# Preparing the next block's tokens earlier: the load in the first pair's value pass, the four sums two and two

## The chip, the cores and the metric

The kernel runs on one core of one Trainium2 chip. The metric is the time of one execution in device microseconds, as a median of several runs. One execution is also recorded by the hardware profiler; its rows are what this document reads. The engines are named as in the rows: PE is TensorE's matrix multiplication, PEld its weight load, DVE is VectorE, ACT is ScalarE, POOL is GpSimd, and SP is SyncE, whose queue issues all the DMAs here.

## The reference

Eight sequences of 3008 tokens with 256 channels go through a spectral mixing layer and then through a gated network. The part around the change is the second one:

```python
X = np.fft.rfft(x, axis=1)                 # then complex 256 x 256 mixing, soft threshold
y = np.fft.irfft(Y, n=x.shape[1], axis=1)
x = y.reshape(24064, 256)
g = x @ w_gate                             # 256 x 1536
silu = g * (1.0 / (1.0 + np.exp(-g)))
val = x @ w_val                            # 256 x 1536
return (silu * val @ w_out).astype(np.float32)   # 1536 x 256
```

## The kernel before

**Two stages.** A first stage of some 680 us does the transforms (by matrix multiplications) and writes the mixed tokens, channels first, to `xt_d` in DRAM. The second stage, `gated_ffn`, fills the rest. It is the stage that the change touches.

**Blocks, pairs, passes.** The second stage runs over 24 blocks of tokens: 22 of 2 x 512 tokens and two of 2 x 384 (`BLOCKS`). Each block runs over six pairs (`q` = 0 to 5) of 256 hidden columns, and each pair has a gate pass (`n` = 0) and a value pass (`n` = 1). In this text the first pair is q = 0 and blocks count from 0.

**Seven products in place of eight.** A pass multiplies a 2 x 2 split of the weights (two halves of the channels, two of the hidden columns) with the 2 x 2 split of the tokens (two halves of the channels, two of the tokens) by a scheme with seven block products, so the operands are seven sums and differences of the quarters. Each product is made of three multiplications, since each operand is split into a high part and a low part, the remainder (`product`, line 516). The gate pass also runs three, the value pass four of the seven products of the down projection of the pair before (`down`).

**Who makes the operands.** For the up projection, `x_sum` (line 502) makes four further operands in place in the token tile `xf`, each a subtraction on GpSimd. `x_part` then makes the high part on ScalarE (line 510) and the low part on GpSimd (line 511), seven times per block. For the down projection, the quarters H11, H12, H22, H21 lie in `hidden`; VectorE makes four differences T1 to T4 in `more` (`diff`, line 527), ScalarE the high parts (`upper`, line 532) and GpSimd the low parts (`lower`, line 536). Seven such low parts fall to a pair: T1, H11 and H22 in the value pass, and H21, T3, T2 and T4 in the gate pass that follows.

**The order.** In the second stage the order on TensorE, VectorE, ScalarE and GpSimd is the order in which the program is written (`manual_schedule`). SyncE's queue is not in that list; the framework's planner orders its requests. Preparation of block b + 1 is woven into block b through a table: `later(ahead, q, n, after, fn)` calls `fn` in pass (q, n) of the block ahead, after the up product numbered `after` (1, 5, 6, 2, 7, 3, 4 is the order in a pass). In a value pass, what stands "after 6" comes on GpSimd's queue behind the low part of T1 and in front of those of H11 and H22.

**The token tile.** There is one tile `xf` (one buffer). `load_x(blk)` may overwrite it once the last of the seven `x_part` of the block before has read it; these stand in the value passes of the fourth pair (two), the fifth (two) and the sixth (three). The weights of the up projection come pass by pass in a ring of four tiles, requested by `load_unit` at the start of each pass for the pass three further on (line 480).

**The inverse pieces.** In blocks 1 to 16 a last piece of the inverse transform is worked off: `inverse` puts eight small multiplications into the gate pass of the third pair, behind ScalarE's reading of the first bank.

Of the kernel before, what the change touches and what calls it, by code (L numbers as in the profile page):

```python
# [120 lines left out]
@with_exitstack  # L121
def spectral_ffn(ctx: ExitStack, tc: tile.TileContext, xp, w_r, w_i, cb, wup_raw, wdn_raw, ca, cf, ci, co, out):
    nc = tc.nc
    const = ctx.enter_context(tc.tile_pool(name="const", bufs=1))
    dram = ctx.enter_context(tc.tile_pool(name="dram", bufs=2, space=DRAM))
    wdn = [const.tile([P, NQ, 7, P], F32R, name=f"wdn_{p}") for p in ("hi", "lo")]
    ring = ctx.enter_context(tc.tile_pool(name="ring", bufs=RING, reuse_waits="tile"))
    xt_d = [dram.tile([P, 2, SEQ], F32, name=f"xt_d{b}", bufs=1) for b in range(B)]
    d2 = {B - 1: dram.tile([NK, P, C], F32, name="d2_last", bufs=1)}
    wup_d = [dram.tile([P, 2, 7 * P], F32, name=f"wup_d{u}", bufs=1) for u in range(2 * NQ)]  # L130


    front = ctx.enter_context(tc.tile_pool(name="front", bufs=1))
    ps_ = ctx.enter_context(tc.tile_pool(name="ps", bufs=1, space=PSUM))

    with ExitStack() as tail:
        last = tail.enter_context(tc.tile_pool(name="last", bufs=2, side="right"))
        with ExitStack() as one:
            finish = transform(one, tc, front, last, ps_, xp, w_r, w_i, cb, wup_raw, wdn_raw, ca, cf, ci, co, wdn, wup_d, xt_d, d2)
        finish()  # L140
        ffn = gated_ffn(ctx, tc, front, ring, ps_, co, wdn, wup_d, xt_d, d2[B - 1], out)
        next(ffn)
    next(ffn, None)
# [319 lines left out]
def gated_ffn(ctx, tc, front, ring, ps_, co, wdn, wup_d, xt_d, d2, out):  # L463
# [22 lines left out]
    def load_x(blk):  # L486
        s, h = BLOCKS[blk]
        end = s + 2 * h
        raw = raws[blk] = front.tile(XF, F32, name="xf", tag="xf").rearrange("p a b -> p (a b)")[:, : 8 * h].rearrange("p (a b) -> p a b", b=h)
        x4 = raw[:, :4, :].rearrange("p a b -> p (a b)").rearrange("p (cc t) -> p cc t", cc=2)  # L490
        at = 0
        while s < end:
            b, off = divmod(s, SEQ)
            n = min(SEQ - off, end - s)
            nc.sync.dma_start(x4[:, :, at : at + n], xt_d[b][:, :, off : off + n])
            s += n
            at += n
        xs[blk] = {}

    def x_sum(blk, o, a, b):  # L500
        f = lambda i: raws[blk][:, i, :]
        g.tensor_tensor(f(o), f(a), f(b), op=ALU.subtract)

    SUMS = ((4, 0, 1), (6, 2, 4), (5, 2, 0), (7, 3, 6))

    def x_part(blk, n_):
        h = BLOCKS[blk][1]
        src = raws[blk][:, X_AT[n_], :]
        part = xs[blk][n_] = sb.tile([P, 2, T], F32R, name="x_parts", bufs=12)
        act.copy(part[:, 0, :h], src)  # L510
        g.tensor_tensor(part[:, 1, :h], src, f32(part[:, 0, :h]), op=ALU.subtract)  # L511
# [209 lines left out]
    def later(blk, q, n, after, fn):  # L721
        todo.setdefault((blk, q, n), {}).setdefault(after, []).append(fn)

    for blk in range(1, len(BLOCKS)):
        ahead = blk - 1
        order = list(X_AT)
        later(ahead, 1, 0, 1, lambda blk=blk: load_x(blk))
        for i, (q, n) in enumerate(((2, 1), (2, 1), (2, 1), (3, 1))):
            later(ahead, q, n, 6, lambda blk=blk, i=i: x_sum(blk, *SUMS[i]))
        for n_, (q, after) in zip(order, ((3, 6), (3, 6), (4, 6), (4, 6), (5, 1), (5, 5), (5, 6))):  # L730
            later(ahead, q, 1, after, lambda blk=blk, n_=n_: x_part(blk, n_))
    for blk, u in pieces.items():
# [86 lines left out]
```

## Time and profile before

| what | value |
|---|---|
| median of 3 runs | 2769.14 us (2768.75 to 2771.31) |
| time of the profiled execution | 2764.52 us |
| its span, first to last instruction | 2762.6 us |
| mean granted TensorE clock | 0.991 |
| TensorE busy | 2684.7 us (97%) |
| VectorE, ScalarE, GpSimd busy | 2157.9, 1718.8, 2096.8 us (78%, 62%, 76%) |

A busy share is an average over the whole span. In the rows of a timeline, the first number is the start of an instruction in microseconds from the span's start, the second the time that it and its like took; "x3" is three in a row, and the bracket is the time in which the engine was idle just before, with what ended it.

### The profile page before, as it was taken

The page shows a single profiled execution, that of the slowest core. Times are in us where ns is not written, and L with a number is a line of the kernel's source. Part 1 is how long each engine was busy: PE and PEld are TensorE (multiplying, and loading weights), DVE is VectorE, ACT ScalarE, POOL GpSimd, SP SyncE. Part 2 cuts the span into 40 slices and gives each one's busy share as a digit, 9 for nine tenths or more (in the row PEclk, how much of TensorE's full clock was granted, in tenths as well). Part 3 has the DMA queues.
Part 4 walks back from the last instruction along what each step waited for, and adds up shares of the span by engine and source line. Part 5 has one row for each costly group of instructions (what it writes and reads, how often), then busy time and mean ns, then how long its engine had stood idle before and what let it go on. Part 6 is the DMA issues. An engine that isn't in the chain of part 4 may idle for free. (4 is left out here: it accounts for less than half of the span.)

```text
span 2762.6 us, 39633 instructions
## 1 busy us (share of the span) xinstructions
PE 2684.7 (97%) x13173; PEld 2200.4 (80%) x13173; DVE 2157.9 (78%) x2916; ACT 1718.8 (62%) x3280; POOL 2096.8 (76%) x1574
## 2 busy tenths in 40 slices
PE   8999999889999999999999999999999999999998
PEld 5777787787888888888888888888888888888898
DVE  3777677774788888888788878888788888888887
ACT  4666666666656665666665665666666666666665
POOL 1555556554888888888888898889888898888885
PEclk9999999999999999999999999999999999999999
DMA  8889987765344444444444444454444444444453
GB/s 248 263 269 296 305 295 245 235 208 181 134 162 158 155 151 146 167 157 152 139 160 169 152 153 144 159 169 140 148 161 155 162 141 144 152 163 149 148 179 108
DMA packets 180124, 491.88 MB, mean 178 GB/s; under 512 B 17264, under 2 KB 89584, under 8 KB 179824
## 3 DMA queue, kind: packets, MB, share of 16 engines
q1 hardware_dynamic: 179920, 489.35, 53.5%
q8 instruction: 105, 1.72, 0.3%
q14 instruction: 99, 0.81, 0.1%
HBM read 378.65 MB, written 110.62 MB: 177 GB/s over the span
## 5 line engine op out<-in xcount | busy, mean ns | idle before, releaser
L516 PE MATMUL bank<-x_parts,wup 128*128 128x512 f32 (+1 forms) x6048 | 1530.6, 387 | 1.2 <-POOL x_parts L511 0.7
L516 PEld LDWEIGHTS bank<-x_parts,wup 128*128 128x128 f32 x6048 | 1122.6, 188 | 239.2 <-DVE bank L645 22.3
L536 POOL TENSOR_TENSOR h_parts<-more,h_parts 128x512 fp32r<-128x512 f32 (+1 forms) x573 | 846.3, 1492 | 97.8 <-ACT h_parts L532 84.2
L536 POOL TENSOR_TENSOR h_parts<-hidden,h_parts 128x512 fp32r<-128x512 f32 (+1 forms) x432 | 602.9, 1408 | 210.1 <-ACT h_parts L532 167.3
L516 PE MATMUL bank<-h_parts,wdn_hi 128*128 128x512 f32 (+1 forms) x2016 | 627.2, 389 | 2.1 <-POOL h_parts L536 0.9
L532 ACT CAST h_parts<-hidden 128x512 fp32r<-128x512 f32 (+1 forms) x432 | 265.1, 614 | 451.8 <-DVE hidden L618 451.8
L516 PEld LDWEIGHTS bank<-h_parts,wdn_hi 128*128 128x128 f32 x2016 | 378.1, 188 | 97.3 <-POOL h_parts L536 26.3
L618 DVE TENSOR_TENSOR hidden<-hidden,bank 128x512 f32<-128x512 f32 (+1 forms) x576 | 375.9, 674 | 77.8 <-PE bank L516 69.2
L557 DVE TENSOR_TENSOR sums<-sums,bank 128x512 f32<-128x512 f32 (+1 forms) x360 | 241.8, 672 | 228.5 <-PE bank L516 228.4
L532 ACT CAST h_parts<-more 128x512 fp32r<-128x512 f32 (+1 forms) x576 | 351.7, 611 | 103.6 <-DVE more L527 94.9
L516 PE MATMUL bank<-h_parts,wdn_lo 128*128 128x512 f32 (+1 forms) x1008 | 388.9, 386 | 4.2 <-DVE sums L557 4.2
L527 DVE TENSOR_TENSOR more<-hidden 128x512 f32<-128x512 f32 (+1 forms) x288 | 341.0, 1222 | 0.0
L616 ACT ACTIVATE hidden<-bank 128x512 f32<-128x512 f32 (+1 forms) x432 | 252.1, 583 | 85.5 <-PE bank L516 79.4
L527 DVE TENSOR_TENSOR more<-hidden,more 128x512 f32<-128x512 f32 (+1 forms) x288 | 284.5, 988 | 0.0
L351 POOL TENSOR_TENSOR t<-t,y 128x512 f32<-128x512 f32 x96 | 132.5, 1380 | 132.6 <-DVE y L350 132.6
L623 ACT COPY bank<-bank 128x512 f32<-128x512 f32 (+1 forms) x288 | 161.6, 561 | 109.4 <-DVE hidden L618 104.0
L645 DVE TENSOR_TENSOR bank<-hidden,bank 128x512 f32<-128x512 f32 (+1 forms) x288 | 196.3, 681 | 37.2 <-PE bank L516 27.4
L516 PEld LDWEIGHTS bank<-h_parts,wdn_lo 128*128 128x128 f32 x1008 | 189.5, 188 | 41.2 <-issue 4.5
L511 POOL TENSOR_TENSOR x_parts<-xf,x_parts 128x512 fp32r<-128x512 f32 (+1 forms) x168 | 210.5, 1272 | 11.5 <-PE bank L516 7.1
L316 POOL TENSOR_TENSOR f<-f 128x256 f32<-128x256 f32 x96 | 84.0, 875 | 149.7 <-ACT f L315 146.7
L631 ACT COPY hidden<-bank 128x512 f32<-128x512 f32 (+1 forms) x288 | 167.3, 581 | 2.6
L349 ACT COPY t<-mixb 64x256 f32<-64x256 f32 x384 | 140.6, 366 | 25.9 <-PE mixb L337 16.2
(94 smaller groups left out, 3280.4 us busy)
## 6 DMA issues: line engine op xcount, KB each, us to landing
wup<-wup_d SPq DMA_DIRECT2D x288, 896.0 KB, 4.6
d<-a SPq DMA_DIRECT2D x128, 192.0 KB, 4.3
a_in<-d SPq DMA_DIRECT2D x96, 256.0 KB, 4.4
out<-o SPq DMA_DIRECT2D x88, 256.0 KB, 6.1
scratch<-xp SPq DMA_DIRECT2D x116, 192.0 KB, 4.8
d<-z SPq DMA_DIRECT2D x84, 256.0 KB, 3.9
z_in<-d SPq DMA_DIRECT2D x56, 384.0 KB, 5.2
xt_d<-xt SPq DMA_DIRECT2D x56, 376.0 KB, 4.4
```

Of the source, the lines that this page charges most:

```text
L349: nc.scalar.copy(t[64 * half : 64 * half + 64, k * C : (k + 1) * C], mixb[64 * k : 64 * k + 64, half * C : (half + 1) * C])
L511: g.tensor_tensor(part[:, 1, :h], src, f32(part[:, 0, :h]), op=ALU.subtract)
L516: nc.tensor.matmul(o, lhsT=weights[w], rhs=parts[x], start=start and i == 0, stop=stop and i == 2, skip_group_check=True)
L527: v.tensor_tensor(at(o, h), at(a, h), at(b, h), op=ALU.subtract)
L532: act.copy(pair[i][:, 0, :h], at(i, h))
L536: eng.tensor_tensor(pair[i][:, 1, :h], at(i, h), f32(pair[i][:, 0, :h]), op=ALU.subtract)
L557: v.tensor_tensor(o, o, spare[:, :h], op=ALU.add)
L616: act.activation(at(i, h), src, AF.Silu)
L618: v.tensor_tensor(at(i, h), at(i, h), src, op=ALU.mult)
L623: act.copy(b3[:, :h], b1[:, :h])
L631: act.copy(m5, b2[:, :h])
L645: v.tensor_tensor(b2[:, :h], m5, b3[:, :h], op=ALU.add)
```

## The change

Three lines of the table `later` change. The load of the next block's tokens moves from the gate pass of the second pair to the value pass of the first. The four sums, which stood as three in the value pass of the third pair and one in that of the fourth, now stand as two in the value pass of the second pair and two in that of the third. Their place in the pass (after product 6) and their own order stay, as do the seven token parts.

```diff
     for blk in range(1, len(BLOCKS)):
         ahead = blk - 1
         order = list(X_AT)
-        later(ahead, 1, 0, 1, lambda blk=blk: load_x(blk))
-        for i, (q, n) in enumerate(((2, 1), (2, 1), (2, 1), (3, 1))):
-            later(ahead, q, n, 6, lambda blk=blk, i=i: x_sum(blk, *SUMS[i]))
+        later(ahead, 0, 1, 1, lambda blk=blk: load_x(blk))
+        for i, q in enumerate((1, 1, 2, 2)):
+            later(ahead, q, 1, 6, lambda blk=blk, i=i: x_sum(blk, *SUMS[i]))
         for n_, (q, after) in zip(order, ((3, 6), (3, 6), (4, 6), (4, 6), (5, 1), (5, 5), (5, 6))):
             later(ahead, q, 1, after, lambda blk=blk, n_=n_: x_part(blk, n_))
```

## Rows read from the trace of the kernel before

**Rows 1.** The page: busy time of each engine, share of the span, instructions.
```profile
PE 2684.7 (97%) x13173; PEld 2200.4 (80%) x13173; DVE 2157.9 (78%) x2916; ACT 1718.8 (62%) x3280; POOL 2096.8 (76%) x1574
```

**Rows 2.** Waits of PEld, 700 to 2741 us: total us, times, longest us.
```profile
PEld bank L516 <- POOL h_parts L536: 24.7, 69, 0.5
PEld bank L516 <- DVE bank L645: 21.5, 66, 0.4
```

**Rows 3.** Timeline of ACT: line 623 at the start of blocks 1, 17, 21, 22.
```profile
765.02 0.57 ACT L623 COPY bank<-bank 128x512 f32<-128x512 f32 x1 [0.74 <-DVE hidden L618]
...
2177.19 0.57 ACT L623 COPY bank<-bank 128x512 f32<-128x512 f32 x1 [0.74 <-DVE hidden L618]
...
2525.59 0.57 ACT L623 COPY bank<-bank 128x512 f32<-128x512 f32 x1 [0.74 <-DVE hidden L618]
...
2611.38 0.46 ACT L623 COPY bank<-bank 128x384 f32<-128x384 f32 x1 [0.74 <-DVE hidden L618]
```

**Rows 4.** Timeline of ACT, block 19: line 623 opening pairs three to six.
```profile
2380.18 0.57 ACT L623 COPY bank<-bank 128x512 f32<-128x512 f32 x1 [0.74 <-DVE hidden L618]
...
2394.45 0.57 ACT L623 COPY bank<-bank 128x512 f32<-128x512 f32 x1 [0.74 <-DVE hidden L618]
...
2409.45 0.57 ACT L623 COPY bank<-bank 128x512 f32<-128x512 f32 x1 [0.74 <-DVE hidden L618]
...
2424.28 0.57 ACT L623 COPY bank<-bank 128x512 f32<-128x512 f32 x1 [0.74 <-DVE hidden L618]
```

**Rows 5.** Timeline of POOL, block 19, from the third pair's value pass.
```profile
2390.01 3.93 POOL L502 TENSOR_TENSOR xf<-xf 128x512 f32<-128x512 f32 x3
2393.90 4.70 POOL L536 TENSOR_TENSOR h_parts<-hidden,h_parts 128x512 fp32r<-128x512 f32 x3
```

**Rows 6.** Timeline of PEld, block 19, fourth pair's gate pass.
```profile
2395.24 0.19 PEld L516 LDWEIGHTS bank<-h_parts,wdn_hi 128*128 128x128 f32 x1 [0.21 <-POOL h_parts L536]
...
2396.94 0.19 PEld L516 LDWEIGHTS bank<-h_parts,wdn_hi 128*128 128x128 f32 x1 [0.49 <-POOL h_parts L536]
...
2398.10 0.53 PEld L516 LDWEIGHTS bank<-x_parts,wup 128*128 128x128 f32 x3 [0.39 <-DVE bank L645]
```

**Rows 7.** Timeline of DVE, block 19: gate passes of pairs four and six.
```profile
2394.28 3.15 DVE L527 TENSOR_TENSOR more<-hidden 128x512 f32<-128x512 f32 x2
...
2424.11 1.95 DVE L527 TENSOR_TENSOR more<-hidden 128x512 f32<-128x512 f32 x2
2426.30 0.69 DVE L645 TENSOR_TENSOR bank<-hidden,bank 128x512 f32<-128x512 f32 x1 [0.24 <-PE bank L516]
```

**Rows 8.** Timeline of POOL, block 19, fifth pair's value pass and what follows.
```profile
2419.83 2.54 POOL L511 TENSOR_TENSOR x_parts<-xf,x_parts 128x512 fp32r<-128x512 f32 x2
2422.33 2.57 POOL L536 TENSOR_TENSOR h_parts<-hidden,h_parts 128x512 fp32r<-128x512 f32 x2
2426.05 1.30 POOL L536 TENSOR_TENSOR h_parts<-hidden,h_parts 128x512 fp32r<-128x512 f32 x1 [1.15 <-DVE more L527]
```

**Rows 9.** Timeline of POOL, block 19, second pair's value pass and what follows.
```profile
2377.42 1.29 POOL L536 TENSOR_TENSOR h_parts<-hidden,h_parts 128x512 fp32r<-128x512 f32 x1 [1.64 <-ACT h_parts L532]
2379.51 1.29 POOL L536 TENSOR_TENSOR h_parts<-hidden,h_parts 128x512 fp32r<-128x512 f32 x1 [0.81 <-ACT h_parts L532]
2381.94 1.29 POOL L536 TENSOR_TENSOR h_parts<-hidden,h_parts 128x512 fp32r<-128x512 f32 x1 [1.14 <-ACT h_parts L532]
```

**Rows 10.** Timeline of ACT, block 9: line 623 opening pairs three and four.
```profile
1499.73 0.57 ACT L623 COPY bank<-bank 128x512 f32<-128x512 f32 x1 [0.75 <-DVE hidden L618]
...
1515.26 0.57 ACT L623 COPY bank<-bank 128x512 f32<-128x512 f32 x1 [0.75 <-DVE hidden L618]
```

**Rows 11.** Timeline of SP around the start of block 20.
```profile
2437.78 0.32 SPq L480 DMA_DIRECT2D wup<-wup_d  x1
2438.15 0.83 SPq L495 DMA_DIRECT2D xf<-xt_d  x1
```

**Rows 12.** DMA issues: count, KB each, median us from issue to landing.
```profile
wup<-wup_d SPq DMA_DIRECT2D x288, 896.0 KB, 4.6
...
xf<-xt_d SPq DMA_DIRECT2D x15, 1024.0 KB, 6.9
```

## The prediction

> **What bounds the kernel now.** I read first the table of engines, then the waits of TensorE's weight loader, then the lengths of the passes, and last what each engine does inside the passes that are too long.
>
> TensorE is busy for 97% of the span [rows 1], so in the gated network nearly every microsecond is its own. What an edit of GpSimd's order can give back is only the time in which TensorE stands still for GpSimd. The waits of the weight loader over the gated network name two causes of nearly equal size: 69 waits for a low part that GpSimd makes (24.7 us), and 66 for the bank that VectorE adds at line 645 (21.5 us) [rows 2]. That is three of each per block in 22 blocks. These totals overstate the loss, since the loader runs ahead of the multiplications and makes up part of it; I therefore go by lengths.
>
> ScalarE's copy at line 623 runs once per pass, so the distance from one such copy to another is a length. The rows give the starts of blocks 1, 17, 21 and 22 (counted from 0) [rows 3]. Blocks 1 to 16 take (2177.19 - 765.02) / 16 = 88.26 us each. Blocks 17 to 20 take (2525.59 - 2177.19) / 4 = 87.10 us. Block 21 takes 2611.38 - 2525.59 = 85.79 us. Block 21 does the same multiplications on 512 columns, but the tokens that it prepares for its successor are only 384 wide. It is the control: a block whose GpSimd work fits.
>
> Inside a block between 17 and 20 the third pair takes 2394.45 - 2380.18 = 14.27 us, the fourth 15.00 and the fifth 14.83 [rows 4]. So the loss sits in the fourth and fifth pairs: 0.73 + 0.56 = 1.29 us, against 87.10 - 85.79 = 1.31 by the control.
>
> Why there: in the value pass of the third pair GpSimd does three sums in a row (3.93 us), and only then, back to back, three subtractions in 4.70 us [rows 5]. The first of these ends at about 2395.2, and the loader resumes at 2395.24 after 0.21 us of waiting for it; the second ends at about 2396.9, and the loader resumes at 2396.94 after 0.49 us; then it waits 0.39 us for VectorE's bank [rows 6]. VectorE is late as a consequence: two differences took it 3.15 us in that gate pass, where the gate pass behind only two extra instructions shows 1.95 us [rows 7]. The fourth pair's value pass has three extras too (one sum and two token parts), and the fifth pair pays 0.56 us. The fifth pair's value pass has exactly two extras, 2.54 us in all, and two subtractions follow in 2.57 us; after them GpSimd is already idle again for 1.15 us [rows 8]. Two extras fit; three do not.
>
> **The change, part by part.**
>
> *The sums.* Nothing is removed: 4 sums per block, about 3.93 / 3 = 1.31 us each [rows 5]. What changes is extras per value pass. Second to fifth pair, before: 0, 3, 3, 2. After: 2, 2, 2, 2. The last pair keeps its 3 token parts, which end the block and lie inside the control's 85.79 too.
>
> *The second pair's value pass, which gains two sums.* Today GpSimd is idle there for 1.64 us, 0.81 us and 1.14 us around three subtractions [rows 9]. The subtraction in front of the first gap is over at 2377.42 - 1.64 = 2375.8. Two sums follow to about 2378.4 (the second reads what the first wrote; I allow 0.1 us for it). The subtraction of H11 then runs until 2379.7, where it now ends at 2378.7. That of H22 starts at about 2379.7 instead of 2379.51 and ends near 2381.0, 0.1 to 0.2 us late. The next is due at 2381.94, so the delay is repaid before it. Is TensorE waiting by then? In the fourth pair, without its waits, the loader would have wanted H11 at 0.79 - 0.21 = 0.58 us after the pass began, and H22 at 2.49 - 0.49 - 0.21 = 1.79 us after it [rows 4, 6]. The third pair's gate pass begins at 2380.18 [rows 4]: H11 would be ready 0.5 us before that, H22 0.8 us after it, about 1 us of margin for each. I cost the two sums at nothing. The cover is that idle time; if it were gone, the cost would be what three extras cost, 0.73 us per block.
>
> *The third pair's value pass, which loses one of three sums,* becomes the same case: the fourth pair falls from 15.00 to about 14.27 us.
>
> *The fourth pair's value pass* keeps only two token parts, the case of [rows 8]: the fifth pair falls from 14.83 to 14.27 us.
>
> *The load.* It is written one pass earlier, and the only transfer that it is moved past is one request for weights. In the trace it already runs earlier than either place: SyncE's own order puts it at 2438.15, right behind the weight request at 2437.78 [rows 11], before the block even begins. It takes 6.9 us to land [rows 12], so the tokens are there by 2445.1. Pairs last 14.3 us, so the first sum in the new place comes some 24 us after the block's start at about 2438.5. Even if the load went out only at its written place, 7 us into the block, it would land with some 10 us in hand. A cost of nothing is the lower bound; the upper one is in the slower rival.
>
> *What is late next.* The blocks with an inverse piece (1 to 16) lose time of another kind: in one of them the third pair takes 1515.26 - 1499.73 = 15.53 us [rows 10], 1.26 us over 14.27. This is not touched by the change and stays. Without it these blocks take 88.26 - 1.26 = 87.00 us, 1.21 above the control.
>
> **The sum.** Blocks 1 to 16: 16 x 1.21 = 19.4 us. Blocks 17 to 20: 4 x 1.31 = 5.2 us. Blocks 0 and 22 also do full preparation (22 is narrower, preparing the same width); I take 1.3 each, 2.6 us. Together 27.2 us. The profiled execution took 2764.52 us and would take 2737.3; the median of the runs shown, 4.6 us higher at 2769.14, becomes 2742.
>
> **The rivals.**
>
> *The inverse piece meets the two sums* (chance 0.07). In blocks 1 to 16 the gate pass behind the moved sums also holds the inverse, whose multiplications stand in TensorE's own order. If the late H22 reaches it, the third pair pays what the fourth pays now: 16 x 0.73 = 11.7 us, a gain of 15.5 us, 2754 us. Against it: the margin of about 1 us.
>
> *VectorE is held by the later subtraction* (chance 0.08). The difference at the end of a value pass reads two SBUF tiles and slows beside GpSimd [rows 7]. If the 0.1 to 0.2 us by which H22 is late goes on to VectorE and from there to TensorE in the third and fourth pair, it costs up to 2 x 0.15 x 22 = 6.6 us: 2749 us. Against it: in the gate pass behind two extras VectorE still had 0.24 us to wait for TensorE [rows 7], which covers it. The Trainium skill, "SBUF — State Buffer", section "Who interferes with whom", says that a VectorE instruction with two SBUF inputs contends with a GpSimd instruction that reads SBUF and that the one issued first blocks the other for its whole length. By that rule sums added to a pass are a danger to VectorE's differences. The trace agrees that differences stretch (1.95 us to 3.15 us for two).
>
> *The burst only moves* (chance 0.05). If two sums in a row behave like three because the second depends on the first, the third and fourth pairs pay what the fourth and fifth pay now: no change, 2769 us. For it: sums are not token parts, and no pass of before holds just two. Against it: both kinds last the same (3.93 / 3 and 2.54 / 2 us).
>
> *Slower: the load holds SyncE's queue* (chance 0.03). If the load is queued in front of a weight request and waits there for the previous tokens' last reader, the weights come late. A request goes out three passes (about 21.4 us) before its use and lands in 4.6 us [rows 12], so a hold of 16.8 us is free. Past 18.0 us each block loses more than the 1.24 us it gains. At 20 us it would lose 3.2 us in each of 22 blocks, 70 us, and end at 2812 us. Against it: the load follows the preceding request by 0.37 us [rows 11], so its wait is over when it reaches the queue's head.
>
> **How the numbers follow.** The forecast, that both late pairs return to 14.27 us, has 0.77. It alone would give 2738 to 2745: at best blocks fall to six pairs of 14.27 us, 85.62, some 0.17 x 22 = 3.7 us more; at worst a tenth of the gain stays behind. The range takes in the two rivals that keep part of the gain, and about 1 us either way for the runs' scatter (2768.75 to 2771.31): 2736 to 2754. A change under 0.2% (5.5 us) can't be told from none. Faster: 0.77 + 0.08 + 0.07 = 0.92; same 0.05; slower 0.03.
>
> **What would show it.** Right: the waits of the weight loader for GpSimd's parts and for line 645 fall from three each per block to one each; the fourth and fifth pairs take 14.27 us; blocks 17 to 20 take about 85.8 us and blocks 1 to 16 about 87.0; the sums stand two and two, and GpSimd's idle time before the gate pass's first subtraction is back at about 1.1 us in the third, fourth and fifth pairs. Wrong: a third pair over 14.27 us in blocks 17 to 20, or over 15.53 us in blocks 1 to 16 (the first two rivals); waits of the loader for weight transfers (the slower one).

## The result, and the profile after

The changed kernel takes 2740.43 us (median of 4 runs, 2739.0 to 2741.13); the kernel before took 2768.94 us in the runs beside it. The ratio is 0.9895, with a 95% interval from 0.9877 to 0.9913: 28.5 us less, between 24 and 34. The forecast was 2742 us. The second stage ran at a granted clock of 1.00 (the upper level, 2.4 GHz) in both profiles, so the clock is not the difference.

The waits of TensorE's weight loader in the gated network, from 700 to 2720 us, are few now (total us, times, longest us):

```profile
PEld bank L706 <- ACT hidden L616: 7.9, 16, 0.5
PEld bank L516 <- DVE bank L645: 4.6, 22, 0.2
PEld bank L516 <- ACT bank L623: 0.8, 4, 0.2
PEld bank L516 <- POOL h_parts L536: 0.3, 1, 0.3
```

The 69 waits for GpSimd's low parts are down to one, and the 66 for VectorE's bank to 22 [rows 2]. What heads the list now, the inverse piece (line 706), was there before and was not touched.

The lengths, read again from ScalarE's copy at line 623 (its timeline): first the starts of blocks 1, 17, 21 and 22, then those of pairs three to six in block 19.

```profile
767.50 0.57 ACT L623 COPY bank<-bank 128x512 f32<-128x512 f32 x1 [0.74 <-DVE hidden L618]
...
2160.00 0.57 ACT L623 COPY bank<-bank 128x512 f32<-128x512 f32 x1 [0.74 <-DVE hidden L618]
...
2503.13 0.57 ACT L623 COPY bank<-bank 128x512 f32<-128x512 f32 x1 [0.74 <-DVE hidden L618]
...
2588.89 0.46 ACT L623 COPY bank<-bank 128x384 f32<-128x384 f32 x1 [0.75 <-DVE hidden L618]
...
2360.25 0.57 ACT L623 COPY bank<-bank 128x512 f32<-128x512 f32 x1 [0.74 <-DVE hidden L618]
...
2374.53 0.57 ACT L623 COPY bank<-bank 128x512 f32<-128x512 f32 x1 [0.74 <-DVE hidden L618]
...
2388.81 0.57 ACT L623 COPY bank<-bank 128x512 f32<-128x512 f32 x1 [0.74 <-DVE hidden L618]
...
2403.09 0.57 ACT L623 COPY bank<-bank 128x512 f32<-128x512 f32 x1 [0.74 <-DVE hidden L618]
```

Blocks 1 to 16 take (2160.00 - 767.50) / 16 = 87.03 us, where they took 88.26 [rows 3]. Blocks 17 to 20 take 343.13 / 4 = 85.78, where they took 87.10. Block 21, the control, is unchanged (85.76 and 85.79), and blocks 17 to 20 have come down to it; blocks 1 to 16 stay 1.27 us above, with their inverse piece. In block 19 the third, fourth and fifth pairs take 14.28 us each; the fourth and fifth took 15.00 and 14.83 [rows 4]. The third did not grow.

Nor did it grow with an inverse piece, where a late GpSimd was the first rival. These copies open the third and fourth pairs of block 9; the third pair takes 15.53 us, as before [rows 10].

```profile
1492.41 0.57 ACT L623 COPY bank<-bank 128x512 f32<-128x512 f32 x1 [0.74 <-DVE hidden L618]
...
1507.94 0.57 ACT L623 COPY bank<-bank 128x512 f32<-128x512 f32 x1 [0.74 <-DVE hidden L618]
```

GpSimd in block 19, from the second pair's value pass, the pass that gained two sums (timeline; the pass ends at 2360.25):

```profile
2354.56 1.29 POOL L536 TENSOR_TENSOR h_parts<-more,h_parts 128x512 fp32r<-128x512 f32 x1 [0.83 <-ACT h_parts L532]
2355.81 2.66 POOL L502 TENSOR_TENSOR xf<-xf 128x512 f32<-128x512 f32 x2
2358.43 2.56 POOL L536 TENSOR_TENSOR h_parts<-hidden,h_parts 128x512 fp32r<-128x512 f32 x2
2362.01 1.29 POOL L536 TENSOR_TENSOR h_parts<-hidden,h_parts 128x512 fp32r<-128x512 f32 x1 [1.03 <-ACT h_parts L532]
```

The sums lie in what were gaps of 1.64 and 0.81 us [rows 9], and 1.03 of the 1.14 us of idle time in front of the next subtraction is left: the two sums made GpSimd 0.11 us late, and that was repaid.

VectorE in the gate passes of the third pair, which comes behind the first two moved sums, and of the fourth (timeline):

```profile
2360.08 2.06 DVE L527 TENSOR_TENSOR more<-hidden 128x512 f32<-128x512 f32 x2
2362.26 0.70 DVE L645 TENSOR_TENSOR bank<-hidden,bank 128x512 f32<-128x512 f32 x1
...
2374.36 1.95 DVE L527 TENSOR_TENSOR more<-hidden 128x512 f32<-128x512 f32 x2
2376.54 0.70 DVE L645 TENSOR_TENSOR bank<-hidden,bank 128x512 f32<-128x512 f32 x1 [0.23 <-PE bank L516]
```

In the fourth pair the two differences take 1.95 us instead of 3.15, and for line 645 it is VectorE that waits for TensorE again, as behind two extras before [rows 7]. In the third pair GpSimd's 0.11 us went on to VectorE: the differences take 2.06 us. But line 645 still begins 2.01 us into the pass, as in the fourth pair; of the 0.23 us of slack there, 0.12 are left, and TensorE lost nothing.

One profiled execution is not a clean measure of the whole. The span fell by 23.8 us (2762.6 to 2738.8), less than the medians did, since the first stage, which the change leaves alone, took 3.8 us longer in this execution. The second stage can be measured by itself, from the first to the last copy at line 623. These are that line's rows, of after and of a second profile of the same kernel:

```profile
L623 ACT COPY bank<-bank x288: 463/570/579, 682.8 to 2717.7; 128x512 f32<-128x512 f32 x132, 128x384 f32<-128x384 f32 x12
```

```profile
L623 ACT COPY bank<-bank x288: 463/570/575, 682.9 to 2717.9; 128x512 f32<-128x512 f32 x132, 128x384 f32<-128x384 f32 x12
```

That is 2034.9 and 2035.0 us. The same row of the kernel before says 679.0 to 2741.5, or 2062.5 us. The second stage lost 27.6 us, against a forecast sum of 27.2. The experiments below are compared by this length too.

### The profile page after: what moved, and what is told of

Same layout as the page of the kernel before. It is cut to its first block, busy times and chain, and to the rows that moved or that the text cites. A ratio compares the mean times of both kernels' runs of the same rounds, so it can differ in the third digit from the quotient of the medians.

```text
span 2738.8 us, 39634 instructions
## 1 busy us (share of the span) xinstructions
PE 2655.4 (97%) x13173; PEld 2207.0 (81%) x13173; DVE 2087.3 (76%) x2916; ACT 1712.2 (63%) x3280; POOL 2061.7 (75%) x1574
## 5 line engine op out<-in xcount | busy, mean ns | idle before, releaser
L536 POOL TENSOR_TENSOR h_parts<-hidden,h_parts 128x512 fp32r<-128x512 f32 (+1 forms) x432 | 565.1, 1316 | 204.0 <-ACT h_parts L532 164.5
L516 PE MATMUL bank<-h_parts,wdn_hi 128*128 128x512 f32 (+1 forms) x2016 | 613.5, 385 | 0.9 <-POOL h_parts L536 0.9
L527 DVE TENSOR_TENSOR more<-hidden 128x512 f32<-128x512 f32 (+1 forms) x288 | 293.0, 1056 | 0.0
L527 DVE TENSOR_TENSOR more<-hidden,more 128x512 f32<-128x512 f32 (+1 forms) x288 | 258.6, 898 | 0.0
```

Of the source, the lines that this page charges most:

```text
L516: nc.tensor.matmul(o, lhsT=weights[w], rhs=parts[x], start=start and i == 0, stop=stop and i == 2, skip_group_check=True)
L527: v.tensor_tensor(at(o, h), at(a, h), at(b, h), op=ALU.subtract)
L536: eng.tensor_tensor(pair[i][:, 1, :h], at(i, h), f32(pair[i][:, 0, :h]), op=ALU.subtract)
```

## The experiments

All are compared with the kernel before on the same chip. The table gives the median, the ratio with its interval, and the length of the second stage in the profiled execution. Each ratio is to runs of before beside that kernel, whose medians lie between 2768.1 and 2769.8 us.

| kernel | median us | ratio to before | second stage us |
|---|---|---|---|
| before | 2768.94 | 1 | 2062.5 |
| the change | 2740.43 | 0.9895 [0.9877, 0.9913] | 2034.9 |
| the change again | 2740.70 | 0.9901 [0.9883, 0.9919] | 2035.0 |
| load alone | 2767.69 | 0.9993 [0.9983, 1.0003] | 2063.3 |
| sums alone | 2738.76 | 0.9884 [0.9869, 0.9900] | 2035.1 |
| half a sum more, twice | 2746.09 | 0.9915 [0.9898, 0.9931] | 2039.5 |
| a whole sum more, twice | 2769.79 | 1.0001 [0.9991, 1.0012] | 2063.2 |
| three and one | 2749.95 | 0.9934 [0.9917, 0.9951] | 2045.4 |
| four in one pass | 2790.49 | 1.0081 [1.0066, 1.0096] | 2081.7 |
| inverse later | 2737.89 | 0.9889 [0.9874, 0.9905] | 2029.9 |
| spread over six passes | 2741.61 | 0.9904 [0.9888, 0.9920] | 2033.2 |
| both of these | 2736.38 | 0.9886 [0.9867, 0.9905] | 2027.9 |

**Load alone** (against the kernel before):

```diff
-        later(ahead, 1, 0, 1, lambda blk=blk: load_x(blk))
+        later(ahead, 0, 1, 1, lambda blk=blk: load_x(blk))
```

> The load is moved as in the change; the four sums stay three and one. If the gain comes from how many sums stand in one value pass, nothing changes against the kernel before: about 2769 us, the fourth pair at 15.00 us and the fifth at 14.83. If tokens that arrive earlier are worth something, the time falls, by up to the whole 28 us.

**Sums alone** (against the changed kernel):

```diff
-        later(ahead, 0, 1, 1, lambda blk=blk: load_x(blk))
+        later(ahead, 1, 0, 1, lambda blk=blk: load_x(blk))
```

> The sums are moved as in the change; the load keeps its old place in the second pair's gate pass, one pass before the first sum. If the count of sums per pass is all, 2740 us as with the whole change, fourth and fifth pair at 14.28 us. If the earlier load is needed, GpSimd waits for the tokens in the second pair's value pass, that pair grows over 14.28 us and part of the gain is missing.

The load alone gives nothing that can be told from no change, the sums alone give the whole gain. The reason is on SyncE's queue. This is its timeline around the start of block 19 with the sums alone, where the load is written in the second pair's gate pass; the block starts at about 2326.6:

```profile
2325.81 0.32 SPq L480 DMA_DIRECT2D wup<-wup_d  x1
2326.18 1.26 SPq L495 DMA_DIRECT2D xf<-xt_d  x2
2332.71 0.33 SPq L480 DMA_DIRECT2D wup<-wup_d  x1
```

And with the whole change, where it is written a pass earlier; the block starts at about 2331.6:

```profile
2330.83 0.32 SPq L480 DMA_DIRECT2D wup<-wup_d  x1
2331.20 1.82 SPq L495 DMA_DIRECT2D xf<-xt_d  x2
2337.70 0.33 SPq L480 DMA_DIRECT2D wup<-wup_d  x1
```

In both the load goes out 0.37 us behind the weight request before the block, as in the kernel before [rows 11]. SyncE's queue has the same order for either place of the line, so the moved line moved nothing. That does not hold for every place: one pass earlier still it did move the load, as the run spread over six passes shows.

**Half a sum more, twice** (against the changed kernel; the last sum of each of the two value passes is repeated on its first 256 columns):

```diff
-    def x_sum(blk, o, a, b):
-        f = lambda i: raws[blk][:, i, :]
+    def x_sum(blk, o, a, b, n=None):
+        f = lambda i: raws[blk][:, i, :n]
...
             later(ahead, q, 1, 6, lambda blk=blk, i=i: x_sum(blk, *SUMS[i]))
+            if i in (1, 3):
+                later(ahead, q, 1, 6, lambda blk=blk, i=i: x_sum(blk, *SUMS[i], n=256))
```

> The changed kernel, in which the last sum of each of the two value passes is done again on half its columns (about 0.65 us more of GpSimd work in the second and in the third pair's value pass; the values stay the same). By the first theory the two low parts of H11 and H22 are all that matters, with about 1 us of margin each: 2740 us, third and fourth pair unchanged. By the rival, VectorE's difference at the end of the value pass is held by GpSimd's later subtraction and hands the delay on to TensorE: some 0.65 - 0.24 = 0.4 us per pass, 44 passes, 17 us more, about 2758 us, with VectorE's bank as the only thing that the weight loader waits for.

The second stage grew by 4.6 us and the median by 5.7, so neither number held: the first theory said nothing, the rival 17 us. The mechanism is the rival's. Waits of the weight loader over the gated network:

```profile
PEld bank L516 <- DVE bank L645: 17.2, 66, 0.4
PEld bank L706 <- ACT hidden L616: 4.9, 16, 0.3
PEld bank L516 <- POOL h_parts L536: 1.4, 6, 0.3
```

TensorE waits for GpSimd's parts 6 times, but for VectorE's bank 66 times. Timelines of GpSimd and of VectorE in block 19, around the start of the third pair's gate pass at 2363.04:

```profile
2358.59 3.48 POOL L502 TENSOR_TENSOR xf<-xf 128x512 f32<-128x512 f32 x3
2362.03 4.70 POOL L536 TENSOR_TENSOR h_parts<-hidden,h_parts 128x512 fp32r<-128x512 f32 x3
```

```profile
2362.87 2.71 DVE L527 TENSOR_TENSOR more<-hidden 128x512 f32<-128x512 f32 x2
2365.50 0.68 DVE L645 TENSOR_TENSOR bank<-hidden,bank 128x512 f32<-128x512 f32 x1
```

The three subtractions run through without a gap and take 4.70 us for three, 1.57 each, where two of them took 2.56 in the changed kernel. Beside them VectorE's two differences take 2.71 us instead of 2.06, and line 645 begins 2.46 us into the pass instead of 2.01. So what gives way first is not the date of H11 or H22 but VectorE beside GpSimd. The price is small: in this block the third pair takes 14.51 us, 0.23 more, and the fourth 14.40, 0.12 more. In block 9, where the third pair holds an inverse piece, it is 0.03 and 0.09.

**A whole sum more, twice** (the same edit with `n=None`):

> As the run with half a sum more, but the sum is repeated on all its columns: three extras in the second pair's value pass and three in the third's. If an extra is an extra wherever it stands, the third and the fourth pair pay 0.73 us each as the fourth did before: 22 x 2 x 0.73 = 32 us more than the change, about 2772 us. If the inverse piece in the third pair's gate pass hides the lateness in blocks 1 to 16, the third pair there stays at 15.53 us and the sum is 22 x 0.73 + 6 x 0.73 = 20 us, about 2761 us; if it makes it worse, over 2772 us.

The second stage grew by 28.3 us and gave the gain back; 32 were expected. A repeated sum as third extra costs what a different one did: in block 19 the third pair takes 15.06 us and the fourth 14.97, 0.78 and 0.69 more, where the fourth and the fifth paid 0.72 and 0.55 before. With a piece the third pair grew too: in block 9 it takes 16.10 us instead of 15.53, 0.57 more. The piece hides a part, not all.

**Three and one, and four in one pass** (against the changed kernel; the second edit has `(1, 1, 1, 1)`):

```diff
-        for i, q in enumerate((1, 1, 2, 2)):
+        for i, q in enumerate((1, 1, 1, 2)):
```

> Three sums in the second pair's value pass and one in the third's: extras 3, 1, 2, 2. One overloaded pass, so half of what the kernel before paid: 22 x 0.55 to 0.73 = 12 to 16 us over the change, 2752 to 2756 us, all of it in the third pair. If one large surplus cost no more than two small ones are worth, or the inverse piece in the same pass took it in, it would be under 2750 us.

> All four sums in the second pair's value pass: extras 4, 0, 2, 2 from the second pair to the fifth. If GpSimd's lateness is handed on in full, the third pair pays 0.73 us for the third extra and another 1.3 us for the fourth, 22 x 2.0 = 44 us: about 2784 us. If the pass makes up part of it, between 2756 us (nothing for the fourth) and that.

Three and one cost 10.5 us over the change by the second stage's length (9.5 by the medians), under the 12 to 16 expected. Line 623 in the timeline of ScalarE, opening pairs three and four of blocks 9 and 19, gives the reason:

```profile
1494.44 0.57 ACT L623 COPY bank<-bank 128x512 f32<-128x512 f32 x1 [0.74 <-DVE hidden L618]
...
1510.38 0.57 ACT L623 COPY bank<-bank 128x512 f32<-128x512 f32 x1 [0.74 <-DVE hidden L618]
...
2366.83 0.57 ACT L623 COPY bank<-bank 128x512 f32<-128x512 f32 x1 [0.74 <-DVE hidden L618]
...
2381.80 0.57 ACT L623 COPY bank<-bank 128x512 f32<-128x512 f32 x1 [0.74 <-DVE hidden L618]
```

Without a piece (block 19) the third pair takes 14.97 us, 0.69 over 14.28. With one (block 9) it takes 15.94, only 0.41 over 15.53. Time lost to GpSimd and time lost to the piece overlap here. The loader's waits at the piece fit this, 4.2 us in all instead of 7.9, or 0.23 us less per piece:

```profile
PEld bank L706 <- ACT hidden L616: 4.2, 16, 0.3
```

Four in one pass cost 46.8 us over the change by the second stage's length (50.1 by the medians), and make the kernel slower than before; 44 were expected. The weight loader's waits name the part and its longest wait:

```profile
PEld bank L516 <- POOL h_parts L536: 52.4, 47, 1.9
PEld bank L706 <- ACT hidden L616: 7.9, 16, 0.5
```

The third pair takes 16.38 us in block 19 (from 2403.39 to 2419.77) and 17.65 in block 9, that is 2.1 us more in both. Nothing is made up: the fourth sum passes on its whole 1.3 us and a little more. Nor does the piece hide anything now, and the loader's waits at it are back at 7.9 us; why it hides a part of what three extras cost and nothing of what four cost is not shown.

**Inverse later** (against the changed kernel): what is late next, a wait that the change left.

```diff
             add(last, 1)
-            if q == 2 and blk in pieces:
-                inverse(pieces[blk])
         up(b2, 3, False)
         take(H22, last_sum)
         take(H12, b2[:, :h])
+        if gate and q == 2 and blk in pieces:
+            inverse(pieces[blk])
```

> The changed kernel with the inverse piece moved behind the next product in the same gate pass, when ScalarE has long read the bank that the piece writes. If the wait of the loader for that reading (7.9 us in 16 blocks) is what the third pair pays on top of the piece's own eight multiplications (0.97 us of the 1.26), the third pair of blocks 1 to 16 falls from 15.53 to about 15.25 us: 4 to 5 us less in all, about 2736 us. If the wait only covers time in which the next products would have waited anyway, nothing changes; if ScalarE's copy now comes too late for the next pass, that pass grows.

The 16 waits at line 706 are gone from the list, and the third pair of block 9 lasts from 1492.95 to 1508.17:

```profile
1492.95 0.57 ACT L623 COPY bank<-bank 128x512 f32<-128x512 f32 x1 [0.74 <-DVE hidden L618]
...
1508.17 0.57 ACT L623 COPY bank<-bank 128x512 f32<-128x512 f32 x1 [0.74 <-DVE hidden L618]
```

That is 15.22 us, as expected; the second stage is 5.1 us shorter. The medians differ by 2.8 us (2737.89 and 2740.70), inside their intervals.

**Spread over six passes, and both edits** (against the changed kernel; the second run adds the moved inverse piece):

```diff
-        later(ahead, 0, 1, 1, lambda blk=blk: load_x(blk))
-        for i, q in enumerate((1, 1, 2, 2)):
+        later(ahead, 0, 0, 1, lambda blk=blk: load_x(blk))
+        for i, q in enumerate((0, 1, 1, 2)):
...
-        for n_, (q, after) in zip(order, ((3, 6), (3, 6), (4, 6), (4, 6), (5, 1), (5, 5), (5, 6))):
+        for n_, (q, after) in zip(order, ((2, 6), (3, 6), (3, 6), (4, 6), (4, 6), (5, 5), (5, 6))):
```

> The changed kernel with one extra in the first pair's value pass and two in each of the other five (one sum and one token part in the third). The last value pass then has two extras, no longer three. If three extras are why the first pair's gate pass takes 6.99 us where others take 6.92, it falls to 6.92 and the 22 waits for VectorE's bank that are left vanish: 22 x 0.08 = 2 us less, about 2738 us. If the tokens are not there in time for the first sum, the first pair's value pass grows.

> Both edits: if they are independent, 6 to 7 us below the changed kernel, about 2734 us.

With at most two extras in any value pass, the weight loader's waits for VectorE's bank fall from 22 to one:

```profile
PEld bank L516 <- POOL h_parts L536: 0.6, 2, 0.4
PEld bank L516 <- ACT bank L623: 0.6, 3, 0.2
PEld bank L516 <- DVE bank L645: 0.4, 1, 0.4
```

The second stage is 1.7 us shorter, near the 2 expected, and far below what the medians can tell.

Here the load is written in the first pair's gate pass, and this time it did move. SyncE's timeline around the start of block 19, at 2333.05, and the load's own waits in the gated network:

```profile
2331.20 1.19 SPq L495 DMA_DIRECT2D xf<-xt_d  x2
2332.48 6.91 SPq L480 DMA_DIRECT2D wup<-wup_d  x2
```

```profile
SPq L495 <- POOL x_parts L511: 131.9, 22, 6.1
```

The load now stands in front of the weight request and waits there for GpSimd's last token part, 6.0 us per block; in the changed kernel such a wait occurs once in the whole stage. It cost nothing that can be seen: the weight request behind it goes out 0.57 us before the block, where it went out 0.78 us before in the changed kernel, the pairs of block 19 take 14.28 us each, and no wait of TensorE or its loader for weights appears. Only in block 0 do the tokens come late: GpSimd waits 5.4 us for them once, and the second pair there takes 14.67 us instead of 14.19.

Both edits together give the shortest second stage, 2027.9 us, 7.0 below the change: the two effects add. The median, 2736.38 us, is the lowest of all, but its interval overlaps that of the change, and about 2734 was expected; by runs alone the step beyond the change is not settled.

## Why the prediction was right

**What bounds the kernel.** That the loss sits in the fourth and fifth pairs and comes from three extras in a value pass held: take one away from each and both pairs return to 14.28 us; add one to two other passes and the loss is back.

**The sums at no cost in the second pair.** Held. The subtraction of H22 was forecast to be 0.1 to 0.2 us late; GpSimd came 0.11 us late, and its idle time before the next subtraction is 1.03 us. The allowance of 0.1 us for the second sum's reading of the first fits too: these two sums take 2.66 us, the two in the third pair's value pass 2.55.

**The margin of about 1 us.** Too large, though the result did not come to depend on it. It was worked out from the dates at which TensorE wants H11 and H22. The run with half a sum more, about 0.7 us, shows that VectorE's path gives way earlier. The second rival, VectorE held by a later subtraction, is thus a real mechanism. In the changed kernel it has only 0.11 us to pass on, and the 0.23 us of slack behind it covers that, as the prediction argued against this rival; what was really in hand is the 0.12 us left over. The Trainium skill, "SBUF — State Buffer", section "Who interferes with whom", which names VectorE instructions with two SBUF inputs and GpSimd instructions that read SBUF as the pair that contends, agrees with this trace: the two differences took 1.95 us, 2.06 us, 2.71 us and 3.15 us as GpSimd's subtractions moved onto them.

**The load at no cost.** Held, for the reason that the prediction read in [rows 11]: SyncE's own order puts the load in the same place as before. The margin of 10 us was not needed.

**The inverse rival.** It did not arise, since GpSimd was only 0.11 us late. Its price, the same 0.73 us with a piece as without, was too high for three extras: 0.41 against 0.69 us in one run, 0.57 against 0.78 in another. With four there is no such difference, 2.1 us with a piece and without.

**The burst that only moves.** Excluded by the result.

**The queue held by the load.** It did not arise in the changed kernel. The run spread over six passes has its first half: the load stands in front of a weight request and waits 6.0 us per block for the last reader. But that request was not due during the wait and went out only 0.2 us later, far below the 16.8 us that the prediction called free. Weights that come late were not provoked, so the price named for them stays unproven.

**The sum.** 27.2 us forecast, 27.6 measured in the second stage, 28.5 by the medians. By terms: blocks 1 to 16 gave 16 x 1.23 = 19.7 us (19.4 forecast), blocks 17 to 20 gave 4 x 1.32 = 5.3 (5.2), and blocks 0 and 22 gave 1.38 and 1.42 (86.04 to 84.66, 69.20 to 67.78), 2.8 where 2.6 was forecast. One detail of what would show it was off: one wait per block for GpSimd's parts was to remain, and none does; of VectorE's, one per block did.

## What to carry to other kernels

Where an engine feeds a nearly full TensorE from a queue in written order, count its instructions per pass, not its share of the span: GpSimd is busy for 76% before, and for 75% both in the changed kernel and with four sums in one pass; yet two extras in a value pass were free, three cost 0.7 us and four 2.1 us. Look for a stretch of the same kernel in which the surplus happens to fit (here block 21, whose successor is narrower), since its length is what the others can fall to. And before an edit moves a request in the program, see in the trace who orders that queue: here the load's line could be moved by one pass without moving the load, and one pass more put it in front of a weight request.

## What the runs showed of the hardware that was not expected

The busy time of engines fell although they did the same work. VectorE runs 2916 instructions in both kernels and was busy for 2157.9 us before [rows 1]; this is the page's line of after:

```profile
PE 2655.4 (97%) x13173; PEld 2207.0 (81%) x13173; DVE 2087.3 (76%) x2916; ACT 1712.2 (63%) x3280; POOL 2061.7 (75%) x1574
```

VectorE has 70.6 us less, GpSimd 35.1 us less. What an instruction of one loses beside the other is inside its own duration and counts as busy, so a busy share of these two holds contention. Most of VectorE's fall is in its first differences, which fell from 1222 to 1056 ns on the mean over 288 (before, then after):

```profile
L527 DVE TENSOR_TENSOR more<-hidden 128x512 f32<-128x512 f32 (+1 forms) x288 | 341.0, 1222 | 0.0
L527 DVE TENSOR_TENSOR more<-hidden 128x512 f32<-128x512 f32 (+1 forms) x288 | 293.0, 1056 | 0.0
```

In these profiles the scatter between executions lies in the first stage. The second stage repeated to 0.1 us between two profiles of the same kernel, and the kernel with the load alone agrees with before within 0.8 us. The start of the second stage, however, came anywhere between 677.6 us (sums alone) and 693.6 us (both edits); the granted clock of the first stage was 0.97 and 0.95 in these two, that of the second 1.00 in both. For this change, which lies in the second stage, that stage's length in one profile told more than several times of the whole.
